# First batch of x loaded as f32 on two hardware queues and cast on chip, in a fused cross-attention and PReLU layer

## The chip, the cores and the metric

The kernel runs on one core of one Trainium2 chip. Its time is the device time of one execution in microseconds; with several runs, the median. A core has five engines, each with an instruction stream of its own: TensorE (PE) multiplies, VectorE (DVE) and ScalarE (ACT) do elementwise work and empty PSUM, GpSimd (POOL) does elementwise work on SBUF, SyncE (SP) only issues transfers. Transfers (DMAs) run on 16 DMA engines that all queues share. A queue belongs to the engine that issues: SyncE and ScalarE have hardware queues, GpSimd has a software queue. Here only GpSimd's transfers change the type on the way (f32 in HBM to f16 in SBUF).

## What is computed

With 8 batches, 8 heads, 512 tokens, 32 states and 64 values a head, tokens read from states and states read from tokens, and every row then goes through a two-layer PReLU network:

```python
scores = scale * x @ state.T;  a  = softmax(scores);  xread = a @ state
scores2 = scale * state @ x.T; a2 = softmax(scores2); sread = a2 @ x
rows = concat([xread, sread], axis=2)          # 8 * (512 + 32) rows of 512
h = rows @ w_in                                # 512 -> 2048
g = max(h, 0) + alpha * min(h, 0)
out = g @ w_out                                # 2048 -> 512, f32
```

## The kernel before

Inputs are f32, matmuls work on f16. Since `xread` is `a @ state`, the kernel folds the states into the first layer: `m = state @ w_in` for each batch (steps `m`, in four blocks of 512 columns of w_in, L445), evicted to SBUF by `mo` (L467), and `h = m.T @ a.T` directly (steps `F`, or half by half `f`). The rows of `sread` are gathered in `XS` and go through the network at the end as a ninth batch.

The work is a list of steps. The string `ORDER` names them in program order; each engine executes its own instructions in that order, and a wait holds up everything behind it on its engine. Nothing else schedules: the pools are under a manual schedule. A token such as `xt.0.1.0.2` is the step `xt` with its arguments; the last number of many tokens is the PSUM bank ("place") k0 to k5 that it writes, and letters a, v, p choose ScalarE, VectorE or GpSimd for a copy.

Steps for one batch b, in the order in which they need each other:

- `lx` loads x of the batch with a cast (L162); batch 0 has `lx0`, in two halves of four heads (L179). `xt` transposes it on TensorE, four heads and one of two token halves at a time (L281), `xo` evicts (L286). From batch 2 on `xd`, a DMA transpose on SyncE's queue, does both (L273).
- `sc` makes all scores in PSUM (L295). Batch 0 works first in two halves of four heads (`sc.0.0`, `sc.0.1`).
- State softmax for the tokens: `sb` transposes 32x32 blocks on VectorE (L330), `smax` (L336), `ssh` subtracts on GpSimd (L342), `sexp` on ScalarE (L348), `ssum` with the reciprocal on VectorE (L352, L353), `snorm` multiplies on GpSimd (L356), `wb` transposes back (L364). The result is the weights that `F` and `f` stream.
- Token softmax for the states: `tm` (L376), `te` (L387), `tsum` (L397), `tn` on GpSimd (L401), `tt`, a DMA transpose of the result e2T on SyncE's queue (L405), `rd` the matmuls (L420).
- `F.b.jc` (L478) and `f` (L499) make one `h` of 128 of the 2048 hidden values for 512 tokens; `N` (ScalarE, L510) and `G` (VectorE, L518) are the PReLU; `S.b.q.i` (L530) adds two hidden blocks to the output of 128 tokens, `O` evicts (L568) and stores (L571).

`wi` and `wo` load w_in and w_out in four blocks each, on GpSimd's queue, with a cast (L198, L204); `lst` loads the states of batches 1 to 7 (L192), `str` and `sro` transpose and evict them (L232, L263). The states of batch 0 come as f32 on SyncE's queue (L172), are cast (`stc`, L238), transposed (`stt`) and evicted (`sto`, L246). `oma` turns alpha into 1 - alpha, a column for each hidden block (L251, L252). `Z.k.n` multiplies zeros n times on TensorE (L217); its results are not used.

GpSimd's queue begins with x of batch 0 in two halves, then the states, w_in block 0, x of batch 1, w_in block 1. The rest of w_in and w_out and x of batch 2 follow between GpSimd's own steps.

Of the kernel before, what the change touches and what calls it, by code (L numbers as in the profile page):

```python
# [26 lines left out]
S.0.0.1 S.0.1.1 G.0.5 mo.4.0.a.0 tn.0.1 m.0.2.0.3 sc.1 G.0.7 S.0.2.0.5 mo.0.2.a.0 tm.1 m.1.2.0.4  # L27
wo.2 tn.0.0 mo.0.2.a.1 mo.1.2.a.0 S.0.2.1 lx.2 wo.3 sb.1 F.0.6.3 F.0.9.0 mo.1.2.a.1 N.0.6 S.0.2.2
S.0.0.2 N.0.9 G.0.6 S.0.1.2 smax.1 te.1.1 te.1.0 F.0.11.4 G.0.9 ssh.p.1 F.0.8.3 N.0.8 N.0.11 S.0.0.3
S.0.1.3 m.0.3 G.0.8 F.0.10.0 mo.0.3.a.0 N.0.10 sexp.1 S.0.2.3 mo.0.3.v.1 xd.2 G.0.11 G.0.10  # L30
S.0.3.0.3 m.1.3 S.0.3.1 mo.1.3.a.0 F.0.14.4 S.0.2.4 F.0.13.0 N.0.14 tt.0 ssum.1 S.0.0.4 S.0.1.4
S.0.0.5 S.0.3.2 G.0.14 F.0.12.4 N.0.13 G.0.13 F.0.15.0 snorm.p.1 N.0.12 N.0.15 mo.1.3.a.1 wb.1
S.0.3.3 S.0.1.5 S.0.3.4 G.0.12 S.0.2.5 G.0.15 S.0.3.5 F.1.2.4 S.0.2.6 N.1.2 F.1.0.0 tsum.1 S.0.2.7
N.1.0 S.0.1.6 S.0.1.7 G.1.2 O.0.2.a sc.2 m.2.1.4.5 S.0.0.6 O.0.1.a F.1.7.2 mo.2.1.a.0 mo.2.1.a.1
G.1.0 F.1.1.0 tm.2 sb.2 F.1.3.4 N.1.7 S.0.0.7 S.0.3.6 N.1.1 G.1.1 N.1.3 tn.1.0 O.0.0.a te.2.0
F.1.5.5 S.0.3.7 N.1.5 G.1.3 F.1.9.0 S.1.1.0.1 G.1.7 F.1.4.4 smax.2 O.0.3.a S.1.1.1 tn.1.1 G.1.5
rd.0.2 te.2.1 N.1.9 G.1.9 m.2.3 F.1.6.3 N.1.4 rdo.0.a F.1.12.5 N.1.6 lx.3 G.1.4 F.1.13.2 N.1.12
F.1.8.0 G.1.6 G.1.12 S.1.2.0.4 N.1.13 G.1.13 ssh.p.2 N.1.8 S.1.1.2 F.1.11.3 G.1.8 F.1.10.5 N.1.11
S.1.2.1 N.1.10 G.1.11 G.1.10 S.1.2.2 sexp.2 S.1.1.3 ssum.2 F.1.14.2 F.1.15.0 snorm.p.2 mo.2.3.a.0
S.1.1.4 mo.2.3.a.1 S.1.1.5 m.3.2 m.4.2.3.5 N.1.14 tt.1 tsum.2 N.1.15 G.1.14 mo.3.2.a.1 S.1.1.6  # L40
S.1.2.3 S.1.2.4 mo.3.2.a.0 mo.4.2.a.0 G.1.15 mo.4.2.a.1 S.1.2.5 S.1.1.7 xd.3 O.1.1.a m.3.1.2.0
m.2.2.3.5 sc.3 wb.2 tn.2.1 S.1.2.6 S.1.2.7 mo.3.1.a.1 F.2.15.1 S.1.0.0.0 mo.2.2.a.0 mo.3.1.a.0
O.1.2.a lx.4 mo.2.2.a.1 sb.3 N.2.15 S.1.0.1 tm.3 F.2.13.3 N.2.13 G.2.15 S.1.0.2 F.2.4.2 tn.2.0
F.2.2.4 G.2.13 smax.3 N.2.4 F.2.9.5 F.2.0.1 N.2.9 S.1.0.3 S.1.0.4 G.2.9 S.1.0.5 N.2.2 N.2.0 te.3.0
F.2.12.3 S.1.0.6 N.2.12 G.2.2 G.2.4 G.2.0 xd.4 F.2.7.5 G.2.12 S.1.3.0.4 ssh.p.3 sexp.3 N.2.7 ssum.3
S.1.0.7 te.3.1 F.2.3.2 S.1.3.1 F.2.1.1 N.2.3 S.1.3.2 N.2.1 F.2.8.3 G.2.3 S.1.3.3 G.2.1 S.1.3.4
# [59 lines left out]
def kernel(  # L106
# [106 lines left out]
    def zeros(k, n):  # L213
        t = single(k, f"z_{len(zs)}", [128, 128], F32)
        zs.append(t)
        for _ in range(n):
            nc.tensor.matmul(t, zero, zero, start=True, stop=True)  # L217
# [422 lines left out]
```

## Time and profile before

| what | us |
|---|---|
| median of 3 runs (lowest, highest) | 218.81 (218.28, 219.42) |
| the profiled execution's own time | 219.05 |
| its span, first to last instruction | 217.3 |
| TensorE busy | 210.2 |
| VectorE, ScalarE, GpSimd busy | 166.5, 137.6, 71.1 |
| the granted TensorE clock | 1.000 |
| zeros on TensorE (L217), 82 instructions | 7.5 |
| GpSimd's queue, share of 16 DMA engines | 28.2% |

Busy times are added up for each engine over the span; engines run side by side. A line of the timeline has the start, the time, the engine, the line, the operation, what it writes and reads, how many were merged, and in brackets how long the engine was idle before and what ended that. In the rows by slices a digit is the busy share in tenths. DMA rates count the bytes written, so a transfer that casts f32 to f16 counts half of what it reads.

### The profile page before, as it was taken

The numbers are of one execution on the slowest core, as the hardware profiler recorded it, in microseconds if no ns is written. First come the engines' busy times: TensorE is split into PE (matmuls) and PEld (weight loads), VectorE is DVE, ScalarE is ACT, GpSimd is POOL, SyncE is SP. The second block draws the span as 40 slices with busy tenths as digits, with TensorE's granted clock in tenths as the row PEclk, the third lists the DMA queues.
The fourth block names the chain that finished last, engine by engine and source line by source line (L and its number), as shares of the span: only waits on it lengthen the run. The fifth ranks groups of instructions, "written<-read, shape, count | busy, mean of one in ns | idle before, by whom it ended". The sixth has DMA issues, their size and how long they took to land.

```text
span 217.3 us, 4317 instructions
## 1 busy us (share of the span) xinstructions
PE 210.2 (97%) x1698; PEld 104.0 (48%) x1698; DVE 166.5 (77%) x255; ACT 137.6 (63%) x271; POOL 71.1 (33%) x58
## 2 busy tenths in 40 slices
PE   7979999999999999999999999999999999999994
PEld 7753334444443544544444445444454455554453
DVE  2789998899899899798998869977898466665001
ACT  3498984899988848885857937565545346544021
POOL 7491943730943703191336310902500000000000
PEclk9999999999999999999999999999999999999999
DMA  6999999599196494159922311051240111100124
GB/s 88 173 198 208 195 195 176 139 203 136 54 139 147 53 227 111 51 99 193 236 52 100 97 50 51 0 100 48 50 149 9 40 51 48 48 37 11 51 97 145
DMA packets 39716, 23.12 MB, mean 106 GB/s; under 512 B 22144, under 2 KB 35984, under 8 KB 39696
## 3 DMA queue, kind: packets, MB, share of 16 engines
q0 software_dynamic: 12704, 8.62, 28.2%
q1 hardware_dynamic: 26960, 14.23, 26.5%
q8 instruction: 13, 0.21, 0.4%
q14 instruction: 7, 0.06, 0.1%
q10 hardware_dynamic: 32, 0.01, 0.0%
HBM read 17.31 MB, written 8.91 MB: 121 GB/s over the span
## 4 chain that ended last, share of the span: by engine, by line
PE 87%; DMA 8%; POOL 2%; issue 1%; DVE 1%; ACT 0%; POOLq 0%
PE o L530 48%; PE h L478 24%; DMA w_in_sb<-in_moe_w_in_dram 5%; PE m_ps L445 4%; PE h L487 3%; PE o L578 3%; DMA xT<-xg 3%; PE o L550 2%; PE sr_ps L420 2%; PE sc L295 1%; DVE m L467 1%; POOL xg L179 1%; POOL xg L162 0%; PE h L499 0%; POOL w_in_sb L198 0%
## 5 line engine op out<-in xcount | busy, mean ns | idle before, releaser
L530 PE MATMUL o<-w_out_sb,gt 128*128 128x512 f16 x496 | 125.3, 379 | 0.0
L510 ACT ACTIVATE neg<-h 128x512 f32<-128x512 f32 (+1 forms) x144 | 76.9, 577 | 46.9 <-PE h L478 37.4
L518 DVE SCALAR_TENSOR_TENSOR gt<-neg,oma_sb,h 128x512 f16<-128x512 f32 x128 | 89.9, 738 | 15.8 <-ACT neg L510 14.7
L530 PEld LDWEIGHTS <-gt 128*128 128x128 f16 x496 | 47.3, 98 | 55.4 <-issue 3.4
L478 PE MATMUL h<-aT,m 128*128 128x512 f16 x250 | 68.3, 379 | 0.0
L478 PEld LDWEIGHTS <-m 128*128 128x128 f16 x250 | 24.1, 98 | 28.4 <-issue 0.6
L401 POOL TENSOR_SCALAR e<-e,r 128x512 f16<-128x512 f16 x16 | 25.0, 1568 | 21.1 <-DVE r L397 17.5
L467 ACT CAST m<-m_ps 128x512 f16<-128x512 f32 x50 | 27.0, 603 | 5.0 <-PE m_ps L445 4.6
L356 POOL TENSOR_TENSOR an<-ts,r 128x1024 f16<-128x1024 f32 (+1 forms) x9 | 15.5, 1720 | 33.9 <-DVE r L353 14.8
L342 POOL TENSOR_TENSOR ts<-ts,mx 128x1024 f32<-128x1024 f32 (+1 forms) x9 | 15.5, 1721 | 28.5 <-DVE mx L336 28.5
L568 ACT COPY osb<-o 128x512 f32<-128x512 f32 x22 | 12.9, 591 | 14.9 <-PE o L530 14.9
L445 PE MATMUL m_ps<-w_in_sb,stT 64*32 64x512 f16 x256 | 11.3, 383 | 0.9 <-DMA w_in_sb<-in_moe_w_in_dram 0.7
L387 ACT ACTIVATE e<-sc,nb 128x512 f16<-128x512 f32 x16 | 11.1, 700 | 1.1 <-DVE nb L379 1.1
L364 DVE STREAM_TRANSPOSE aT<-an 128x1024 f16<-128x1024 f16 (+1 forms) x9 | 10.1, 1120 | 1.8 <-POOL an L356 1.8
L518 DVE SCALAR_TENSOR_TENSOR gs<-neg,oma_sb,h 128x256 f16<-128x256 f32 x16 | 7.5, 478 | 4.5 <-ACT neg L510 4.5
L467 DVE CAST m<-m_ps 128x512 f16<-128x512 f32 x14 | 9.1, 679 | 2.1 <-ACT m L467 1.6
L352 DVE TENSOR_REDUCE r<-ts 128x32 f32<-128x1024 f32 (+1 forms) x9 | 9.9, 1095 | 0.0
L336 DVE TENSOR_REDUCE mx<-ts 128x32 f32<-128x1024 f32 (+1 forms) x9 | 9.8, 1092 | 0.0
L376 DVE TENSOR_REDUCE nb<-sc 128x2 f32<-128x1024 f32 x8 | 9.6, 1204 | 0.3 <-PE sc L295 0.3
L487 PE MATMUL h<-XS,w_in_sb 128*128 128x256 f16 x64 | 9.4, 273 | 0.0
L588 DVE COPY osr<-o 128x512 f32<-128x512 f32 x1 | 0.7, 691 | 11.3 <-PE o L578 11.3
L217 PE MATMUL z<-zero 128*128 128x128 f16 x82 | 7.5, 262 | 1.4 <-DVE zero L211 1.1
(51 smaller groups left out, 127.0 us busy)
## 6 DMA issues: line engine op xcount, KB each, us to landing
out_dram<-osb SPq DMA_DIRECT2D x27, 256.0 KB, 2.2
xg<-in_x_dram POOLq DMA_DIRECT2D x7, 512.0 KB, 6.8
w_in_sb<-in_moe_w_in_dram POOLq DMA_DIRECT2D x4, 512.0 KB, 9.3
w_out_sb<-in_moe_w_out_dram POOLq DMA_DIRECT2D x4, 512.0 KB, 8.8
out_dram<-osb SPq DMA_DIRECT2D x9, 128.0 KB, 2.0
xg<-in_x_dram POOLq DMA_DIRECT2D x2, 256.0 KB, 4.2
out_dram<-osr SPq DMA_DIRECT2D x2, 256.0 KB, 3.1
st<-in_state_dram POOLq DMA_DIRECT2D x1, 224.0 KB, 4.8
```

The lines of the kernel that those rows point to most:

```text
L342: engine(e).tensor_tensor(ts, ts, over_blocks(cols(live["mx", b], j, S // N)), ALU.subtract)
L356: engine(e).tensor_tensor(blocks(cols(live["an", b], j, S)), blocks(cols(live["ts", b], j, S)), over_blocks(cols(live["r1", b], j, S // N) ...
L387: nc.scalar.activation(live["e2", b][:, g, :, :], live["sc", b][:, :, :, g, :].rearrange("p r j s -> p (r j) s"), EXP, bias=live["nb", b][ ...
L401: nc.gpsimd.tensor_scalar_mul(e2, e2, live["r2", b][:, g : g + 1])
L445: nc.tensor.matmul(t[N * k : N * (k + 1), :], st_head(b, h)[64 * r : 64 * r + 64, :], w_in_sb[64 * r : 64 * r + 64, c, 512 * f : 512 * (f ...
L467: copier(e)(m_tile(b)[:, f, g, :], live["mp", b, f][g])
L478: nc.tensor.matmul(h.rearrange("p (r j s) -> p r j s", r=2, j=2), ms[b][:, f, g, 128 * j : 128 * (j + 1)], weights(b, g), start=(g == 0), ...
L487: nc.tensor.matmul(h, w_in_sb[:, c, 128 * jc : 128 * (jc + 1)], XS[:, c].rearrange("p q n b -> p (q n b)"), start=(c == 0), stop=(c == n_c ...
L510: nc.scalar.activation(neg, h, RELU, bias=0.0, scale=-1.0)
L518: nc.vector.scalar_tensor_tensor(gt, negs.pop((b, jc)), oma_sb[:, jc : jc + 1], h, ALU.mult, ALU.add)
L530: nc.tensor.matmul(outs[b, q], gts[b, jc][:, 128 * q : 128 * (q + 1)], w_out_sb[:, jc, :], start=(jc == 0), stop=(jc == n_jc - 1),)
L568: copier(e)(osb, t)
```

## The change

- x of batch 0 is loaded as f32 into a buffer of its own (a tile of the pool of m), in four pieces: heads 0 to 2 and 4 to 5 on SyncE's queue, head 3 and heads 6 to 7 on ScalarE's. Steps `xc` cast it to f16: heads 0 to 2 on VectorE, 3 and 4 to 5 on ScalarE, 6 to 7 on GpSimd.
- The states of batch 0 go from SyncE's to ScalarE's queue, with two rows of 64 next to each other for each partition; their eviction undoes that order. alpha goes from ScalarE's to SyncE's queue.
- GpSimd's queue begins with the states of batches 1 to 7, w_in block 0 and x of batch 1; its cast of heads 6 to 7 stands ahead of w_in block 1.
- `Z` multiplies up to 512 columns in one instruction, n counts units of 128 columns. 82 instructions become 21.
- The order of steps is new up to batch 2, and the PSUM places are new in the whole program; from batch 3 on the order is the same. On TensorE `m.1.1` and `m.0.1` stand ahead of the first `f`; on VectorE `ssum.0.1` stands behind `xo.1.0.0`; on GpSimd `tn.0` stands behind `ssh.p.1`; on SyncE `tt.0` stands ahead of `xd.2`.
- The outputs of batch 2 are stored in one transfer instead of two.

```diff
-stc lx0.0 lx0.1 oma id Z.1.20 stt.0 Z.2.18 xt.0.0.0.1 sto.a xt.0.1.0.2 xo.0.0.0.v lst xo.0.1.0.v
-Z.0.6 sc.0.0 xt.0.1.1.3 xt.0.0.1.4 sb.0.0 xo.0.0.1.v smax.0.0 xo.0.1.1.a str.0.5 sc.0.1 str.1.0 wi.0
-sro.0.a lx.1 wi.1 ssh.p.0.0 sb.0.1 Z.1.3 sc.0 Z.5.7 m.0.0.1.2 sro.1.a sexp.0.0 smax.0.1 m.3.0.3.4
-ssh.p.0.1 tm.0 mo.0.0.a.1 sexp.0.1 ssum.0.0 m.1.0.5.0 ssum.0.1 te.0.1 te.0.0 mo.1.0.v.1 wo.0
-mo.1.0.a.0 snorm.p.0.0 mo.3.0.a.1 Z.2.28 xt.1.1.1.2 xt.1.1.0.5 mo.0.0.a.0 snorm.p.0.1 wb.0.0
-mo.3.0.a.0 m.2.0 xt.1.0.1.0 xo.1.1.0.v xt.1.0.0.4 f.0.0.0.1 f.0.1.0.5 wi.2 mo.2.0.a.0 wb.0.1
-mo.2.0.a.1 f.0.1.1 xo.1.0.0.v N.0.1 m.0.1.3.4 f.0.0.1 mo.0.1.a.1 m.1.1 xo.1.1.1.v N.0.0 xo.1.0.1.v
-mo.0.1.v.0 f.0.2.0.2 F.0.3.0 f.0.2.1 F.0.4.3 mo.1.1.v.0 mo.1.1.a.1 F.0.7.4 G.0.1 N.0.2 G.0.0 wo.1
-F.0.5.5 N.0.3 G.0.2 wi.3 m.4.0 N.0.4 S.0.0.0.1 N.0.5 G.0.3 tsum.0 S.0.1.0.2 N.0.7 mo.4.0.a.1 G.0.4
...
+xc.1.a stc lst id xc.0.v wi.0 Z.1.28 stt.0 lx.1 Z.2.8 xt.0.0.0.1 sto.v xc.3.p xo.0.0.0.v xc.2.a oma
+xt.0.1.0.2 xo.0.1.0.a Z.0.5 str.1.3 sc.0.0 sro.1.a xt.0.1.1.4 xt.0.0.1.5 wi.1 xo.0.1.1.a sb.0.0
+str.0.0 xo.0.0.1.v sc.0.1 smax.0.0 m.0.0.1.2 sro.0.a mo.0.0.a.1 wo.0 m.2.0.3.5 mo.0.0.a.0 sb.0.1
+ssh.p.0.0 sc.0 smax.0.1 m.1.0.4.0 ssh.p.0.1 tm.0 sexp.0.0 mo.1.0.a.1 mo.2.0.a.0 sexp.0.1 Z.2.20
+xt.1.0.0.2 xt.1.1.0.1 ssum.0.0 te.0.1 xo.1.0.0.v ssum.0.1 m.3.0.0.3 te.0.0 wi.2 mo.3.0.a.0
+xt.1.0.1.2 mo.3.0.a.1 snorm.p.0.0 mo.2.0.v.1 mo.1.0.a.0 Z.0.18 m.1.1.0.5 wb.0.0 m.0.1 f.0.0.0.3
+snorm.p.0.1 mo.1.1.a.1 wb.0.1 f.0.1.0.4 f.0.1.1 F.0.3.5 mo.1.1.a.0 xo.1.0.1.v xt.1.1.1.2 f.0.0.1
+f.0.2.0.0 N.0.1 mo.0.1.v.0 mo.0.1.a.1 xo.1.1.0.v G.0.1 f.0.2.1 F.0.5.1 N.0.0 N.0.3 m.4.0 xo.1.1.1.v
+wo.1 G.0.0 N.0.2 F.0.4.4 F.0.7.2 S.0.1.0.3 N.0.5 mo.4.0.a.0 wi.3 G.0.3 S.0.0.0.5 G.0.2 N.0.4 G.0.5
...
-    nc.sync.dma_start(st0_32, rows[:n0, :].rearrange("(g p) d -> p g d", p=128))
+    x32 = moe.tile([128, H, 2, 2, D], F32, name="x32", tag="m", bufs=7)
+    heads = ((0, 3), (3, 4), (4, 6), (6, 8))
...
-    nc.scalar.dma_start(al32[:n_jc, :], moe_alpha.rearrange("(jc p) -> jc p", p=128))
+
+    def load_x32(engine, i):
+        lo, hi = heads[i]
+        engine.dma_start(
+            x32[:, lo:hi].rearrange("p k j r d -> p k (j r d)"),
+            x[0, lo:hi].rearrange("k (p j r) d -> p k (j r d)", j=2, r=2),
+        )
+
+    load_x32(nc.sync, 0)
+    nc.sync.dma_start(al32[:n_jc, :], moe_alpha.rearrange("(jc p) -> jc p", p=128))
+    nc.scalar.dma_start(st0_32, rows[:n0, :].rearrange("(p g) d -> p g d", g=2))
+    load_x32(nc.scalar, 1)
+    load_x32(nc.sync, 2)
+    load_x32(nc.scalar, 3)
...
-    def load_x0(g):
...
+    def x0_cast(i, e):
+        lo, hi = heads[i]
+        copier(e)(xgs[0][:, lo:hi], x32[:, lo:hi])
...
-    zero = consts.tile([128, 128], F16)
+    zero = consts.tile([128, 512], F16)
...
-        for _ in range(n):
-            nc.tensor.matmul(t, zero, zero, start=True, stop=True)
+        while n:
+            w = 128 * min(n, 4)
+            nc.tensor.matmul(t[:, :w], zero[:, :128], zero[:, :w], start=True, stop=True)
+            n -= w // 128
...
-        w = 256 if b == 2 else 512
-        for c in range(0, d_model, w):
-            nc.sync.dma_start(rows[:, c : c + w], osb[:, c : c + w])
+        nc.sync.dma_start(rows, osb)
```

More of the change, by code (lines that the diff above doesn't have):

```diff
@@ L29 @@
[L29 to L34, printed above, removed]
@@ new lines @@
+F.1.13.4 xd.3 F.1.10.2 m.2.3 G.1.6 N.1.13 G.1.11 S.1.1.2 N.1.8 ssh.p.2 F.1.14.5 S.1.1.3 N.1.10
+S.1.2.0.3 mo.2.3.a.0 G.1.13 S.1.2.1 sexp.2 G.1.10 S.1.2.2 F.1.15.4 G.1.8 ssum.2 S.1.1.4 mo.2.3.a.1
+S.1.2.3 m.3.2 N.1.14 m.4.2.2.1 G.1.14 mo.4.2.v.0 mo.3.2.a.0 S.1.2.4 N.1.15 snorm.p.2 S.1.1.5
+mo.3.2.a.1 mo.4.2.a.1 S.1.2.5 G.1.15 wb.2 S.1.1.6 S.1.2.6 m.2.2.5.2 m.3.1.4.1 sc.3 S.1.2.7
+mo.3.1.v.0 mo.2.2.a.1 F.2.13.2 lx.4 mo.2.2.a.0 S.1.0.0.4 N.2.13 sb.3 S.1.0.1 F.2.12.5 tsum.2
+mo.3.1.a.1 O.1.2.a S.1.1.7 G.2.13 F.2.4.1 N.2.12 smax.3 S.1.0.2 G.2.12 F.2.9.2 O.1.1.a F.2.2.3 N.2.9
@@ new lines @@
+F.2.15.0 N.2.2 S.1.0.3 tm.3 F.2.0.5 S.1.0.4 tn.1.1 ssh.p.3 N.2.15 S.1.0.5 tt.1 N.2.4 G.2.2 G.2.9
+N.2.0 G.2.15 sexp.3 G.2.0 S.1.0.6 G.2.4 F.2.3.3 F.2.7.2 ssum.3 N.2.7 xd.4 S.1.3.0.0 S.1.3.1 S.1.0.7
+F.2.1.5 tn.2.1 N.2.1 N.2.3 F.2.8.1 G.2.1 S.1.3.2 G.2.3 tn.2.0 S.1.3.3 N.2.8 te.3.1 S.1.3.4 S.1.3.5
+te.3.0 O.1.0.a S.1.3.6 G.2.7 F.2.6.5 N.2.6 m.3.3.3.2 G.2.8 sc.4 rd.1.4 snorm.p.3 F.2.5.1 G.2.6
+mo.3.3.a.0 F.2.14.3 rdo.1.a wb.3 N.2.5 tsum.3 S.2.1.0.5 F.2.11.4 mo.3.3.a.1 G.2.5 S.1.3.7 N.2.14
+F.2.10.2 F.3.4.1 G.2.14 N.2.11 S.2.1.1 F.3.1.3 lx.5 O.1.3.v N.3.4 S.2.1.2 N.2.10 G.2.11 tt.2
@@ new lines @@
+tsum.4 snorm.p.4 F.3.5.3 mo.4.3.a.0 mo.4.3.a.1 F.3.0.5 F.3.10.0 N.3.0 S.2.3.7 O.2.3.a S.2.2.0.2
+S.2.2.1 F.3.11.1 G.3.0 wb.4 S.2.2.2 S.3.3.0.4 F.3.15.5 S.3.3.1 N.3.5 lx.6 G.3.5 te.5.0 te.5.1 N.3.10
+N.3.15 S.2.2.3 F.3.12.3 S.2.2.4 N.3.11 S.3.3.2 lx.7 N.3.12 G.3.10 G.3.15 F.4.6.0 N.4.6 tn.4.0
+F.4.5.5 G.3.11 F.4.3.1 N.4.5 S.2.2.5 G.3.12 G.4.5 S.3.3.3 F.4.4.3 S.3.3.4 F.4.7.5 N.4.4 S.3.3.5
+S.2.2.6 N.4.3 sb.5 N.4.7 S.3.3.6 S.2.2.7 G.4.4 G.4.7 S.3.3.7 F.4.1.3 F.4.0.5 xd.6 O.2.2.a S.3.1.0.2
+O.3.3.a S.3.1.1 F.4.9.4 N.4.1 smax.5 G.4.6 N.4.0 S.3.0.0.0 tn.4.1 S.3.0.1 G.4.1 G.4.0 F.4.8.3
@@ new lines @@
+N.4.14 F.4.12.2 G.4.14 O.3.2.a sexp.6 tn.5.1 S.4.1.0.0 m.6.3 m.7.2.4.5 m.5.2.1.3 mo.6.3.v.0 S.4.1.1
+mo.5.2.v.0 mo.7.2.a.0 S.4.1.2 mo.5.2.a.1 F.5.15.4 mo.6.3.v.1 mo.7.2.a.1 tt.5 S.4.1.3 N.5.15 G.5.15
+F.4.15.1 F.5.12.3 S.4.1.4 F.5.5.5 N.4.12 F.5.13.4 S.4.1.5 N.5.12 N.4.15 G.4.12 tsum.6 G.4.15
+S.4.0.0.2 S.4.1.6 S.4.1.7 N.5.5 S.4.0.1 S.4.2.0.1 O.4.1.v G.5.5 S.4.0.2 F.5.10.0 N.5.13 F.5.1.5
+S.4.2.1 G.5.12 F.5.0.3 N.5.10 S.4.0.3 S.4.2.2 S.4.0.4 G.5.13 tn.6.1 N.5.0 G.5.10 N.5.1 G.5.1
+m.6.1.4.0 m.7.0 mo.6.1.a.1 mo.6.1.a.0 S.4.0.5 mo.7.0.v.0 S.4.0.6 F.5.2.5 N.5.2 S.4.0.7 mo.7.0.v.1
@@ L245, in first_states_out @@
     def first_states_out(e):
-        copier(e)(stT[:, :n0], live.pop("st0_ps").rearrange("d g p -> d (g p)"))
+        copier(e)(
+            stT[:, :n0].rearrange("d (p g) -> d p g", g=2),
+            live.pop("st0_ps").rearrange("d g p -> d p g"),
+        )
     def one_less_alpha():
```

122 lines of the change are left out of this document (50 added, 72 removed).

## The prediction

> **What bounds the kernel now.** I read the engine shares and the slices first, then the chain of work that ended last in order of time, then the DMA queues and the timeline of the first 24 us.
>
> ```profile
> PE 210.2 (97%) x1698; PEld 104.0 (48%) x1698; DVE 166.5 (77%) x255; ACT 137.6 (63%) x271; POOL 71.1 (33%) x58
> ...
> PE   7979999999999999999999999999999999999994
> ```
>
> TensorE is full from the third slice of 5.4 us on. The real matmuls behind the start are the same before and after, so only the moment from which TensorE runs without gaps can move the end, and stalls that the new order makes later. The chain, 0 to 40 us (start, length, what):
>
> ```profile
> 4.82 0.87 POOL xg L162
> 5.68 11.78 DMA w_in_sb<-in_moe_w_in_dram
> 17.46 0.04 issue
> 17.50 0.41 PE m_ps L445 x8
> ```
>
> Up to 17.46 us the chain is the second block of w_in, queued on GpSimd's queue behind x of batch 0, the states, the first block and x of batch 1; after it every step is TensorE's. The DMA view of 0 to 20 us (slices of 0.5 us) says when that queue runs:
>
> ```profile
> DMA  0001416999999999999999999999999999999999
> GB/s 0 0 0 45 103 6 67 179 199 192 196 164 133 165 191 138 174 205 203 207 189 114 168 196 224 186 200 201 205 213 203 201 207 209 207 209 201 209 203 213
> ...
> q0 software_dynamic: 4135, 3.17, 105.9%
> ```
>
> The engines start on it at 3.0 us, need one slice (67 GB/s) to get going, and never rest again; the 64 KB of the first states, on SyncE's queue, came at 1.5 to 2.5 us. The timeline:
>
> ```profile
> 1.23 1.72 POOL L179 DMA_DIRECT2D xg<-in_x_dram  x2 [0.80 <-POOLq L624]
> ...
> 5.84 0.90 PE L281 MATMUL xT_ps<-ident,xg 128*128 128x128 f16 x8
> ...
> 12.39 1.72 PE L217 MATMUL z<-zero 128*128 128x128 f16 x28 [0.28 <-ACT m L467]
> ...
> 15.00 0.62 PE L281 MATMUL xT_ps<-ident,xg 128*128 128x128 f16 x8 [0.88 <-DMA xg<-in_x_dram]
> ...
> 16.35 0.81 PE L499 MATMUL h<-aT,m 128*128 128x512 f16 x3
> 17.50 0.41 PE L445 MATMUL m_ps<-w_in_sb,stT 64*32 64x512 f16 x8 [0.34 <-DMA w_in_sb<-in_moe_w_in_dram]
> ...
> 21.11 1.90 PE L530 MATMUL o<-w_out_sb,gt 128*128 128x512 f16 x8
> ```
>
> x of batch 1 lands at 14.96 us (issued at 4.80), the first `h` starts at 16.35, the first output matmul (S) at 21.11. I take S as the marker: what it gains is gained at the end, unless a later wait eats it.
>
> **The change part by part.**
>
> *x of batch 0 on the hardware queues.* SyncE issued at 0.73 us and its packets ran from about 1.8 (slice 1.5 to 2.0); GpSimd issued at 1.23 and its packets ran from 3.0. So the stream starts 1.1 us earlier; the slow first slice (67 against about 200 GB/s, 0.35 us) now lies under other packets; the 64 KB of states join the stream (+0.2). The transfer itself writes 1 MB of f32 where it wrote 512 KB of f16. No row shows such a load. Below: a w_in block, 1 MB of f32 read, takes 2.54 us (17.46 to 20.0, the next landing). Above: if written bytes were what counts, 1 MB at the 205 GB/s of the cast stream is 5.1 us. The nearest rows are the hardware queue's own between 40 and 60 us:
>
> ```profile
> GB/s 0 0 225 307 365 152 30 73 93 160 123 126 172 236 319 371 339 224 93 195 304 56 4 9 243 291 244 0 0 0 0 0 0 0 0 0 238 287 17 66
> ```
>
> 365 GB/s while only output writes ran: 2.9 us for 1 MB. I take 3.0, against about 3.5 for both halves before (3.0 to 6.5 us). Then x of batch 1 (L) lands 1.1 + 0.35 + 0.5 - 0.2 = 1.75 us earlier, at 13.2; ends 12.7 and 15.3. Everything behind it in GpSimd's queue shifts alike, w_in block 1 to about 15.7.
>
> [...]
>
> *Casts.* Four copies: DVE 768 wide, ACT 256 and 512, GpSimd 512. Rows: 0.28 us for 128 elements on DVE (L238), 0.37 and 0.59 on ACT (L246, L467), 1.05 for a 512-wide two-input op on GpSimd (L342). DVE's is then 0.6 to 0.95, GpSimd's 0.5 to 1.05. Heads 0 to 3 land at 3.5 to 5 us (sharing with the states, which GpSimd issues at 1.23), heads 4 to 7 at 5.2 to 7; cast, 4.4 to 5.9 and 6.1 to 8. The transposes cannot use the early end: the first 28 units of zeros, 107 ns for 128 columns there (20 in 2.31 us, the last one 0.31 long), take 3.0 us from 1.2, and four state transposes (0.42) and 8 more units (0.86) keep TensorE busy to 5.5, against 5.84 before. The first scores come at about 7.2 (7.32 before). What covers all of this is the wait for L: TensorE idles about 1.6 us before it. With heads 4 to 7 a whole us later the cover is gone and 0.4 us shows. GpSimd's cast waits for them with w_in block 1, w_out block 0 and the score shifts queued behind it; the engines are busy with earlier blocks until 13, so the issue at 7 to 9 us costs nothing.
>
> *Zeros.* 82 instructions of 128 columns become 21 of up to 512: 10,496 columns against 10,112. Costs nothing, they stand in waits.
>
> *The new order before S.* TensorE now has both m matmuls of w_in block 1 ahead of the first `h`; DVE has the second half's sum (L352) behind the eviction of batch 1's first transposes, so it waits for L, and with it wait an eviction of m and both transposes back to weights behind it on DVE, and the first `h` that need these. From L: transposes and hop 0.45, eviction 0.42, sum and reciprocal 0.94 (0.69 + 0.25), GpSimd's product 1.04 (L356), transpose back 0.70 (L364), in all 3.55. The w_in way is as long: 2.5 for the block, 0.8 for two m groups, 0.45 for two `h`. Then, to S: `h` matmuls at 0.215 each, 12 of them (2.6), four transposes 0.3, m of batch 4 0.4, switches 0.25: 3.55. S is at L + 7.1 = 20.3, 0.8 us earlier. Before it was 6.15 behind L: what the order gains (the w_in block waits at 17.50) it partly gives to the sum's wait.
>
> *Behind S.* SyncE has the DMA transposes in the other order:
>
> ```profile
> 32.98 3.37 SPq L273 DMA_TRANSPOSE xT<-xg  x1
> 36.40 1.30 SPq L405 DMA_TRANSPOSE e2T<-e  x1
> ```
>
> Now e2T goes first, and it waits for GpSimd's two products (L401, 1.57 each), which moved behind the shift of batch 1 (28.34 before, 1.9 long): shift from 27.6, products to 32.8, e2T issue 1.3, x of batch 2 issued at 34.1. The six such transposes land 5.2 us after issue in the median: 39.3; the first took 6.1, beside the last w_out block (landing at 36.6, now about 35). TensorE gets to the scores that need it (40.43 before) at about 39.2. Cost 0.1, with ends 0 (4.3 us) and 0.9 (6.1 us). Output of batch 2 in one DMA for two: four issues of 0.33 us less on a SyncE that waits; nothing. New PSUM places and the states' layout (512 B rows): nothing, the same sizes are evicted.
>
> **Sum.** -0.8 + 0.1 = -0.7 us. The profiled execution took 219.05 us (span 217.3, 1.75 around it), so 218.35; the median shown is 218.81, 0.24 less than that execution, so 218.1 as a median.
>
> **The rivals.**
> - *Only the start.* The queues take turns without gain: x costs its 3.5 us as before, the slow slice stays, and L moves by the earlier start less the 64 KB alone, 14.96 - 1.1 + 0.2 = 14.06; S at 21.15, no gain, with the 0.1 above 218.9. For it: the cast queue's share is already 105.9%. Against: the 365 GB/s.
> - *More.* Hardware packets fill gaps of the cast stream, x costs 2.5 and heads 4 to 7 land by 6: L at 12.7 or below, w_in block 1 at 15.2, S at 19.7 to 19.9: 217.4. For it: 164 and 133 GB/s at 5.5 to 6.5 us show gaps to fill. Against: S then needs the shift chain of the first half to be on time too.
> - *Late transposes.* x of batch 2 takes 6.1 us again: +0.8 on the forecast, 218.9.
> - *Slower: written bytes count.* x at 205 GB/s takes 5.1 us; L at 15.3, w_in block 1 at 17.8, S at 22.4: +1.3, with the scores' wait 220.2. It decides from 4.1 us for x on (L at 14.3). For it: no row shows an f32 load from HBM of that size, and the cast stream never passes 224 GB/s. Against: 365 for outputs.
>
> **How the numbers follow.** Chances: forecast 0.30, only the start 0.10, late transposes 0.08, more 0.28, slower 0.24. 0.5% of this kernel, 1.1 us, is about what a measurement can tell from no change; the first three lie within it. Faster 0.28, same 0.48, slower 0.24. The range takes in "more" (217.4, 217.0 with its bounds) and "written bytes" (220.2): 217.0 to 220.2; the forecast's own is 217.6 to 218.9.
>
> **What would show it.** Packets of the hardware queues from 1.8 us at over 300 GB/s; batch 1's first transposes at 13.2; the second sum on DVE directly behind them; first `h` at about 16.6 and S at 20.3; e2T issued near 32.8, x of batch 2 near 34.1, its scores waiting little. I am wrong if L comes after 14, if heads 4 to 7 hold up the first-batch softmax, or if TensorE waits at scores 2 for longer than 0.5 us.

## The result and the profile after

The changed kernel takes 219.53 us (22 executions, 219.20 to 222.39) against 218.79 us (22, 218.04 to 219.42): ratio 1.0054, 95% interval 1.0036 to 1.0071. I forecast 218.1, so the sign is wrong; the range (217.0 to 220.2) holds the median. 16 of the 22 lie between 219.20 and 219.67 (median 219.44, so the loss is not the clock's alone); the other six are those with a mean granted TensorE clock of 0.984 to 0.992, and five of them take 220.18 to 222.39. No execution of the kernel before that was timed beside the experiments has a clock below 0.998. The profiled execution is one of the six (220.92, span 219.1), so what belongs to the clock has to be kept apart below.

The page of the kernel after: engine shares, slices and clock.

```profile
PE 209.8 (96%) x1637; PEld 99.4 (45%) x1637; DVE 167.7 (77%) x258; ACT 137.6 (63%) x271; POOL 70.1 (32%) x57
...
PE   7498999999999999999999999999999999999994
...
PEclk9969999999999999999999999999999999999999
```

The second slice (5.4 to 10.9 us) has fallen from 9 to 4 tenths, and the clock is not full in the third. The chain of work that ended last, 0 to 40 us (start, length, what), says what TensorE waits for:

```profile
1.76 7.07 DMA x<-in_x_dram
8.83 0.02 issue
8.85 0.62 ACT xg L194
9.47 0.49 ACT xT L303
9.96 0.04 issue
10.00 0.30 PE sc L312 x8
...
17.37 0.48 ACT m L484
17.86 0.04 issue
17.90 1.15 PE z L230 x5
19.05 0.04 issue
19.09 0.45 PE m_ps L462 x8
```

Before, the chain led through GpSimd's queue to block 1 of w_in and from 17.5 us on through TensorE. Now it starts with heads 4 and 5 of x of batch 0, which land 7.07 us after their issue, goes through their cast on ScalarE to an eviction, also on ScalarE, and only then to the first scores, at 10.00. Between 10 and 17.9 us more than half of it is ScalarE's. And it goes through `z`, zeros. The timeline of TensorE:

```profile
7.03 0.58 PE L246 MATMUL st_ps<-ident,st 128*64 128x128 f16 x14 [0.22 <-DMA st<-in_state_dram]
...
10.00 0.30 PE L312 MATMUL sc<-xT,stT 64*32 64x256 f16 x8 [2.39 <-ACT xT L303]
...
17.90 1.13 PE L230 MATMUL z<-zero 128*128 128x512 f16 x5 [0.87 <-ACT m L484]
19.09 0.63 PE L462 MATMUL m_ps<-w_in_sb,stT 64*32 64x512 f16 x16
19.64 0.82 PE L516 MATMUL h<-aT,m 128*128 128x512 f16 x3
...
23.35 1.97 PE L547 MATMUL o<-w_out_sb,gt 128*128 128x512 f16 x8
```

In the kernel before, the first scores ran at 7.32, on an eviction by VectorE:

```profile
7.32 0.30 PE L295 MATMUL sc<-xT,stT 64*32 64x256 f16 x8 [0.24 <-DVE xT L286]
```

TensorE now waits 2.39 us ahead of the first scores, where it waited 0.24. S is at 23.35 (21.11 before). The DMA view of 0 to 20 us, which shows that the stream as a whole did what was wanted:

```profile
DMA  0002039999999999999999999999999999999998
GB/s 0 0 0 26 0 70 307 362 366 258 237 280 362 356 246 217 213 207 200 195 196 201 200 200 206 206 205 209 209 201 203 213 238 190 193 205 207 209 209 133
```

The stream moves 237 to 366 GB/s from 3.0 to 7.5 us, and x of batch 1 (L) lands at 13.21, block 1 of w_in at 15.74: to the tenth what I had forecast. What failed is that L no longer decides S.

### The profile page after: what moved, and what is told of

It reads as the page before. It is cut to its first block, busy times and chain, and to the rows that moved or that the text cites. A ratio compares the mean times of both kernels' runs of the same rounds, so it can differ in the third digit from the quotient of the medians.

```text
span 219.1 us, 4198 instructions
## 1 busy us (share of the span) xinstructions
PE 209.8 (96%) x1637; PEld 99.4 (45%) x1637; DVE 167.7 (77%) x258; ACT 137.6 (63%) x271; POOL 70.1 (32%) x57
## 4 chain that ended last, share of the span: by engine, by line
PE 85%; ACT 7%; DMA 3%; DVE 2%; issue 1%; SPq 0%
PE o L547 47%; PE h L495 23%; PE m_ps L462 3%; DMA x<-in_x_dram 3%; PE h L504 3%; PE o L593 3%; ACT m L484 2%; ACT neg L527 2%; PE o L567 2%; PE sr_ps L437 2%; ACT e L404 1%; PE sc L312 1%; DVE m L484 1%; DVE ts L345 1%; PE z L230 1%
## 5 line engine op out<-in xcount | busy, mean ns | idle before, releaser
L535 DVE SCALAR_TENSOR_TENSOR gt<-neg,oma_sb,h 128x512 f16<-128x512 f32 x128 | 89.9, 737 | 16.2 <-ACT neg L527 15.4
L484 ACT CAST m<-m_ps 128x512 f16<-128x512 f32 x48 | 26.5, 599 | 7.1 <-PE m_ps L462 6.8
L462 PE MATMUL m_ps<-w_in_sb,stT 64*32 64x512 f16 x256 | 12.2, 405 | 0.7 <-ACT stT L280 0.4
L484 DVE CAST m<-m_ps 128x512 f16<-128x512 f32 x16 | 10.4, 677 | 1.7 <-ACT m L484 1.3
L381 DVE STREAM_TRANSPOSE aT<-an 128x1024 f16<-128x1024 f16 (+1 forms) x9 | 10.1, 1120 | 1.3 <-POOL an L373 1.1
L365 ACT ACTIVATE ts<-ts 128x1024 f32<-128x1024 f32 (+1 forms) x9 | 8.7, 964 | 0.2 <-POOL ts L359 0.2
```

Of the source, the lines that this page charges most:

```text
L462: nc.tensor.matmul(t[N * k : N * (k + 1), :], st_head(b, h)[64 * r : 64 * r + 64, :], w_in_sb[64 * r : 64 * r + 64, c, 512 * f : 512 * (f ...
L484: copier(e)(m_tile(b)[:, f, g, :], live["mp", b, f][g])
L535: nc.vector.scalar_tensor_tensor(gt, negs.pop((b, jc)), oma_sb[:, jc : jc + 1], h, ALU.mult, ALU.add)
```

## The experiments

In each edit the tokens of the order are shown with their neighbours. S is the first output matmul of the profiled execution, as in the prediction.

**1. The eviction ahead of the cast.**

```diff
-xc.3.p xo.0.0.0.v xc.2.a oma xt.0.1.0.2 xo.0.1.0.a Z.0.5
+xc.3.p xo.0.0.0.v oma xt.0.1.0.2 xo.0.1.0.a xc.2.a Z.0.5
```

> The changed kernel with one step moved: on ScalarE the eviction of the first half's second token half stands ahead of the cast of heads 4 and 5. Theory (late heads): heads 4 to 7 land at 8.5 to 8.8 us whatever stands on ScalarE, and the cast held up the first scores, which ran at 10.0. They now run at 7.6 (behind the state transposes that wait for the states at 7.0); the second half's scores, which need heads 4 to 7, come at about 10.8 instead of 11.6, so S comes only 0.7 to 0.9 us earlier than with the same clock before, and the time is 218.5 to 218.9. Rival (order behind): the sums, the m matmuls and the DMA transposes in their new places set the time; 219.4 to 219.6, unchanged. Rival (one wait): the cast ahead of the eviction was all that went wrong; then S = 20.5 to 21 and 217.9 to 218.3.

218.82 us (218.72 to 219.26), ratio to the kernel before 1.0010 (0.9998 to 1.0022). The first scores run at 7.42, the second half's at 10.33, S at 21.53; one of 12 executions has a clock of 0.992. So one token on ScalarE was most of what the change had lost, in part by way of the clock (run 9, which holds the clock and leaves the token where it is, has 1.0034): it is the theory's case, with the time at its upper end. The forecast's 218.1 is still 0.7 away. The chain of this kernel, 0 to 30 us, where TensorE comes in only at 16 us:

```profile
1.75 6.38 DMA x<-in_x_dram
...
8.16 0.62 ACT xg L194
8.78 1.05 ACT stT L280
9.83 0.44 ACT xT L303
10.28 0.97 ACT stT L280
11.25 0.94 ACT m L484 x2
12.19 0.53 ACT ts L365
12.72 0.96 ACT m L484 x2
13.68 0.53 ACT ts L365
14.21 1.34 ACT e L404 x4
15.55 0.48 ACT m L484
...
16.08 1.15 PE z L230 x5
...
17.27 0.45 PE m_ps L462 x8
```

ScalarE works from 8.16 to 16.04 without a gap: a cast, two evictions of states, one of x, five of m, the two exponentials of the first batch (`ts`) and the token softmax's (`e`). L, at 13.2, is in no link of it. And TensorE, which waited for ScalarE, first multiplies zeros for 1.15 us before it makes m of batch 1, whose block of w_in had landed at 15.72.

**2. Ten matmuls of zeros where TensorE was idle.**

```diff
-Z.0.5 str.1.3 sc.0.0
+Z.0.5 str.1.3 Z.0.40 sc.0.0
```

> The changed kernel with 40 more units of zeros on TensorE (10 matmuls 512 wide, 0.21 us each at the full clock) between the state transposes and the first scores, where TensorE was idle from 7.6 to 10.0 us. Nothing else moves. Theory (late heads, clock on top): the first scores still run at 10.0, no execution shows a granted clock below 1, the spread shrinks to 219.1 to 219.7, the median is 219.3 to 219.5: the drop cost only what the executions above 219.8 show. In the profile S is at 22.2 to 22.7. Rival (the clock is all of it): the median falls to 218.2 to 218.7. Rival (the clock falls for another reason than the idle time): executions at 220 to 222 are still there.

220.22 us (219.81 to 220.44), clock 1.000 in all six. The spread is gone, as the theory says, but the median is 0.7 above its 219.3 to 219.5. The reason is in the landings: in this execution heads 4 to 7 landed at 7.74 and 7.92, not 8.5 to 8.8, so the scores could have run near 9 (an estimate: 7.92, the cast of 0.62 and the eviction of 0.49), and the zeros held them to 9.92. Too many zeros; run 9 has fewer.

**3. GpSimd's queue silent until x has landed.**

```diff
-xc.1.a stc lst id xc.0.v wi.0 Z.1.28
+xc.1.a stc id xc.0.v xc.3.p lst wi.0 Z.1.28
```

> The changed kernel with GpSimd's cast of heads 6 and 7 put ahead of all transfers on GpSimd's queue, so that the 1 MB of f32 x, the 64 KB of first states and alpha have the DMA engines to themselves: the disputed cost alone. Theory (shared engines): the hardware queues move 300 KB/us or more, and heads 4 to 7 land at 5.2 to 5.8 us instead of 8.5 to 8.8; the first scores then wait for the states (transposed ahead of them), x of batch 1 lands at 15.5 or later, the time is 220 to 223. Rival (the load is slow by itself, from many short rows or from two queues): heads 4 to 7 land at 7.5 or later with nothing beside them.

One execution: 223.24 us. Heads 6 and 7 land at 6.56, heads 4 and 5 at 6.93: between the two expectations. The DMA view of 0 to 10 us, in slices of 0.25 us, of this kernel:

```profile
GB/s 0 0 0 0 0 0 0 82 64 20 63 217 285 324 377 377 383 379 385 389 334 295 266 131 94 25 0 0 0 0 0 0 0 0 57 79 100 79 151 201
```

and of the changed kernel:

```profile
GB/s 0 0 0 0 0 0 0 51 0 0 4 135 295 320 336 387 387 344 273 244 235 239 226 333 356 367 381 332 254 238 221 213 217 209 209 205 205 195 189 201
```

Alone, the f32 load runs at 377 to 389 GB/s for about 1.5 us, near the rate that I had taken (365). But the packets that come at 1.75 us carry only 20 to 82 GB/s; the load proper begins at 2.75 us, from 5.75 us on it trickles (131, 94, 25 GB/s), and the last piece lands at 6.93. So from first packet (1.78) to last landing it is 5.1 us alone, and beside GpSimd's queue 7 us in the profiled execution (landings at 8.46 and 8.83); in runs 1, 2 and 9, with the same loads, the last landing is at 7.92 to 8.18.

**4. Wide zeros and one store for batch 2, on the kernel before.**

```diff
-    zero = consts.tile([128, 128], F16)
+    zero = consts.tile([128, 512], F16)
...
-        w = 256 if b == 2 else 512
-        for c in range(0, d_model, w):
-            nc.sync.dma_start(rows[:, c : c + w], osb[:, c : c + w])
+        nc.sync.dma_start(rows, osb)
```

> The kernel before with two parts of the change alone: zeros 512 columns wide and the outputs of batch 2 in one transfer. Theory: both cost nothing, 218.5 to 219.1, clock 1.0. Rival (the wide zeros matter, by the clock or by delaying what stands behind them): 219.4 or more, or some executions with a clock below 1.

218.64 us, ratio 1.0003 (0.9986 to 1.0020), clock 0.997 or more: these two parts cost nothing that the interval shows. A side result: here x of batch 1 landed at 14.01 and S was at 20.71, with the same load as before (14.01 in run 6 too). The execution of the kernel before that I had read (L 14.96, S 21.11) was the later one; against this one, L gains 0.8 us by the change and not 1.75.

**5. No zeros ahead of m.1.1,** on top of run 1.

```diff
-mo.2.0.v.1 mo.1.0.a.0 Z.0.18 m.1.1.0.5 wb.0.0
+mo.2.0.v.1 mo.1.0.a.0 m.1.1.0.5 wb.0.0
```

> The changed kernel with the eviction ahead of the cast (as in the run that moved that step alone, 218.82) and, besides, without the 18 units of zeros that stand on TensorE ahead of m.1.1. There TensorE waited for ScalarE until 16.08, multiplied zeros for 1.15 us, and only then made m of batch 1, whose block of w_in had landed at 15.72. Theory (ScalarE is late and the zeros stand behind it, on the path): m.1.1 at 16.1, the first h at 16.8 to 17.0, S at 20.4 to 20.8 instead of 21.53, time 217.8 to 218.2. Rival (the weights from GpSimd and VectorE set the first h, and the evictions of m behind them S): the first h at 17.4 or later, S at 21.1 to 21.5, time 218.5 to 218.9.

218.84 us, ratio 1.0030 (1.0005 to 1.0055), of two groups: seven executions at full clock take 218.26 to 218.91, five with a clock of 0.990 to 0.992 take 219.85 to 220.51. In the profiled one the first h is at 16.72 and S at 20.75, as the theory has it; its time of 217.8 to 218.2 is missed even at full clock (median of the seven: 218.60). So the zeros were on the path, and they were not idle either: without them five of 12 executions have a lower clock, and these take 1.8 us longer (their median is 220.41).

**6. The load undone, the order kept.** The four loads and casts go; `lx0`, as in the kernel before, stands first on GpSimd's queue.

```diff
-xc.1.a stc lst id xc.0.v wi.0 Z.1.28
+stc lx0.0 lx0.1 id lst wi.0 Z.1.28
```

> The changed kernel with the load undone: x of batch 0 again in two halves with a cast, first on GpSimd's queue; the new order, zeros and stores stay, and the four casts on chip go. Theory (the late landing of heads 4 to 7 started the loss, the order with its evictions and zeros ahead of the first h adds to it): heads land at 5.2 and 6.8, the first scores run at 7.4 to 7.6, the second half at 8.9 to 9.3, x of batch 1 lands at 14.6 to 15.0 and block 1 of w_in at 17.1 to 17.5; the first h stands behind m.1.1, which needs that block, so at 18.0, S at 21.6 to 21.9: 219.0 to 219.5. Rival (the load alone made it slower): S at 21.0 to 21.2, 218.4 to 218.8, as before. Rival (the order alone made it slower): S at 22.2 or later, 219.5 or more.

220.55 us, ratio 1.0099 (1.0078 to 1.0120): worse than theory, and the rival "the order alone". S at 22.82; five of six executions have a clock of 0.989 to 0.992, the sixth takes 220.31. I had not seen why: the new order puts a transposition of the later states ahead of the first scores, and with the old load these states land at 8.73.

```profile
8.77 0.58 PE L235 MATMUL st_ps<-ident,st 128*64 128x128 f16 x14 [2.04 <-DMA st<-in_state_dram]
9.29 0.30 PE L301 MATMUL sc<-xT,stT 64*32 64x256 f16 x8
```

The order is made for a queue that begins with the states, so this run gives no price of the order by itself.

**7. Half and half.** Heads 4 to 7 by GpSimd with a cast, first on its queue; no zeros ahead of m.1.1.

```diff
-xc.1.a stc lst id xc.0.v wi.0 Z.1.28
+xc.1.a stc lx0 id xc.0.v lst wi.0 Z.1.28
...
-    load_x32(nc.sync, 2)
-    load_x32(nc.scalar, 3)
```

> The changed kernel with heads 4 to 7 loaded with a cast by GpSimd, first on its queue, and only heads 0 to 3 as f32 on the hardware queues; no casts of heads 4 to 7 on chip, and no zeros ahead of m.1.1. Theory (late heads): with half the f32 rows, heads 4 to 7 land at 6.0 to 6.8, the first scores at 7.4 to 7.6 and those of the second half at 9.0 to 9.5; x of batch 1 at 13.2 to 13.8, S at 20.0 to 20.6, time 217.3 to 218.0. Rival (the hardware queues slow whatever stands beside them, so heads 4 to 7 still come at 7.5 or later): S at 20.8 to 21.4, 218.2 to 218.7.

219.86 us, ratio 1.0070 (1.0045 to 1.0096); two executions at full clock take 219.16 and 219.20, four with 0.990 to 0.992 take 219.64 to 220.85. Heads 4 to 7 land at 6.90, but the first scores run at 9.11: as in run 6 the states (8.56) hold them up. I missed that a second time; both of its theories fell to it.

**8. The new load with the order of before** from the second half's scores on, and 8 units of zeros for 28 ahead of x of batch 1 (the lines of the changed kernel that these replace are left out).

```diff
+xt.0.1.0.2 xo.0.1.0.a Z.0.5 sc.0.0 str.0.5 sb.0.0 sro.0.a xc.2.v smax.0.0 xt.0.1.1.3 xt.0.0.1.4 xo.0.0.1.v
+xo.0.1.1.a sc.0.1 str.1.0 wi.1 ssh.p.0.0 sb.0.1 Z.1.3 sc.0 Z.5.7 m.0.0.1.2 sro.1.a sexp.0.0 smax.0.1
...
+mo.3.0.a.1 Z.2.8 xt.1.1.1.2 xt.1.1.0.5
```

> The new load with the order of before from the second half's scores on (with the start reordered: the eviction ahead of the cast, heads 4 and 5 cast on VectorE, one state transposition and its eviction while TensorE waits for heads 4 to 7; 8 units of zeros instead of 28 ahead of x of batch 1). Theory (the new order's ScalarE work, sums and zeros ahead of the first h are a part of the loss): heads 4 to 7 land at 8.0 to 8.8, the second half's scores at 9.8 to 10.4, x of batch 1 at 13.2, the first h at 15.5 to 16.2, S at 20.0 to 20.6, 217.4 to 218.0. Rival (late heads set everything through the second half's softmax, whatever the order): S at 21.0 to 21.6, 218.4 to 219.0.

220.04 us, ratio 1.0060 (1.0035 to 1.0085): four executions at full clock, 218.46 to 219.14, seven with 0.981 to 0.992, 219.90 to 221.57. S at 20.74, between the two expectations. Full clock or not, this order is no better than that of run 1 (the four at full clock have a median of 218.94, run 1 has 218.82).

**9. Five matmuls of zeros instead of ten,** in the changed kernel.

```diff
-Z.0.5 str.1.3 sc.0.0
+Z.0.5 str.1.3 Z.0.20 sc.0.0
```

> The changed kernel with 20 units of zeros, five matmuls of 0.21 us at the full clock, between the state transposes and the first scores: they end near 8.7 us, ahead of the scores, which come at 9.1 at the earliest. Theory (the clock is granted anew every 3.41 us, by how busy TensorE was in the 3.41 us before; the traces so far show the half clock behind stretches in which it was busy for 0.12 to 0.33, and the full one from 0.38 on): no such stretch is left, no execution has a clock below 0.998, the slow executions of the changed kernel (220 to 222.4) are gone and the rest is as it was: 219.2 to 219.7, median 219.3 to 219.5. Rival (zeros in front of the scores cost time by themselves, as ten matmuls did with 220.2): median 219.8 or more. Rival (the clock falls for something else): executions of 220 and more with a clock near 0.99 remain.

219.56 us (219.28 to 219.83), ratio 1.0034 (1.0019 to 1.0048), all 12 at 0.999 or more. Theory: the executions above 220 are gone, and the rest is where it was, though the median lies just above its 219.5. The shares in the expectation count only the time in which columns stream (512 in about 0.21 us, as the prediction's `h` matmuls at 0.215). In the profile's own busy time, which the view by stretches gives, the same reads like this. Three stretches of 3.41 us of the changed kernel (length, TensorE busy, weight loads, VectorE, ScalarE, GpSimd, clock, DMA):

```profile
4.04:7.46 3.42, 2.44 (x32) 1.23 (x30) 2.19 (x8) 0.41 (x1) 0.18 (x1) 1.00 1.13 301
7.46:10.87 3.41, 1.02 (x24) 0.73 (x20) 0.74 (x3) 2.02 (x4) 2.06 (x3) 1.00 1.31 204
10.87:14.29 3.42, 3.02 (x62) 1.24 (x63) 2.81 (x6) 3.12 (x6) 1.69 (x2) 0.50 1.34 204
```

of run 3, which fell twice over:

```profile
4.71:8.12 3.41, 1.58 (x16) 0.68 (x12) 2.21 (x8) 1.51 (x3) 1.51 (x3) 1.00 0.34 117
8.12:11.53 3.41, 0.41 (x8) 0.41 (x10) 0.00 (x0) 0.00 (x0) 2.97 (x4) 0.50 0.90 129
11.53:14.95 3.42, 3.42 (x58) 2.06 (x52) 1.99 (x4) 2.23 (x3) 0.42 (x1) 0.50 1.24 172
14.95:18.36 3.41, 2.95 (x61) 1.41 (x53) 3.29 (x6) 3.41 (x8) 2.41 (x3) 1.00 1.32 199
```

and one of run 7, which did not fall:

```profile
7.45:10.86 3.41, 1.88 (x44) 1.49 (x45) 1.37 (x4) 1.64 (x3) 0.00 (x0) 1.00 1.25 201
```

In the changed kernel's trace the clock changes at 10.87, 14.29 and 219.09 us, 3.41 and 204.80 us apart: once and 60 times such a stretch. It falls to half behind 1.02 us of work in 3.41 (1.37 in run 6, 1.58 in run 3), at 219.09 behind 0.47, and stays half behind 0.41 (run 3); it is full again behind 3.02 us (3.02 in run 6, 3.42 in run 3). In the other profiles the stretches of this length that I read have 1.88 us (run 7), 1.95 (run 8), 2.00 (run 5) and more, and the clock stays full. The fall begins at 10.87 us here, at 9.54 in run 6, at 8.12 in run 3. Why the same kernel is hit in some executions only is not shown: no two traces here show one kernel both ways.

**10. Zeros where TensorE waits,** on top of run 5.

```diff
-Z.0.5 str.1.3 sc.0.0 sro.1.a xt.0.1.1.4
+Z.0.5 str.1.3 sc.0.0 sro.1.a Z.0.12 xt.0.1.1.4
...
-xt.1.0.1.2 mo.3.0.a.1
+Z.2.16 xt.1.0.1.2 mo.3.0.a.1
```

> The kernel with the eviction ahead of the cast and no zeros ahead of m.1.1 (median 218.84, of two groups: seven executions of 218.26 to 218.91 at full clock and five of 219.85 to 220.51 with a clock of 0.990 to 0.992), now with zeros where TensorE waits: 12 units behind the first scores and 16 units ahead of the last early transposition of batch 1, both ending before what they stand ahead of is ready. Theory (busy share by stretches of 3.41 us): the second group is gone, all executions at 218.2 to 219.0, median 218.4 to 218.7, which is no gain over the kernel before. Rival (the zeros ahead of m.1.1 were only in the way, and the second group has another cause): the second group stays, median near 218.9 or above.

218.32 us (217.86 to 218.87), ratio 0.9973 (0.9961 to 0.9986), clock 0.999 or more in all 12: the second group is gone, as the theory says. The theory's "no gain" is not borne out here, but see run 12. In this execution block 1 of w_in ends a wait again: GpSimd issues it behind the cast of heads 6 and 7, it lands 8.30 us later, and TensorE waits 0.80 us for it ahead of m.1.1:

```profile
7.80 0.56 POOL xg L194
8.36 8.30 DMA w_in_sb<-in_moe_w_in_dram
...
16.71 0.46 PE m_ps L462 x8
```

**11. Half and half once more,** on top of run 10, the state transposition behind the first scores.

```diff
-xo.0.1.0.a xc.2.a Z.0.5 str.1.3 sc.0.0 sro.1.a Z.0.12 xt.0.1.1.4 xt.0.0.1.5 wi.1 xo.0.1.1.a
+xo.0.1.0.a Z.0.5 sc.0.0 Z.0.4 xt.0.1.1.4 xt.0.0.1.5 wi.1 str.1.3 xo.0.1.1.a sro.1.a
...
-sc.0.1 smax.0.0 m.0.0.1.2
+sc.0.1 smax.0.0 Z.2.24 m.0.0.1.2
```

> The kernel with zeros in the waits (median 218.32), with heads 4 to 7 loaded with a cast by GpSimd, first on its queue, as in the half-and-half run, but with the state transposes behind the first scores, so that the states' landing at 8.6 holds up nothing ahead of them; 24 units of zeros fill the wait for block 0 of w_in. Question: does the late landing of heads 4 to 7 (7.7 to 8.2, and two casts) still cost something there? Theory (it does: the second half's softmax sets the weights): heads 4 to 7 land at 6.6 to 7.0, the second half's scores run at 8.9 to 9.3 instead of 10.1 to 10.3, the weights and the first h come 0.3 us or more earlier than 17.27, time 217.7 to 218.1. Rival (ScalarE's row of evictions, and x of batch 1 and block 1 of w_in, which now land 0.5 us later, set the first h): first h at 17.2 to 17.8, 218.3 to 218.9.

218.77 us, ratio 1.0004 (0.9991 to 1.0017). Heads 4 to 7 land at 7.31, the second half's scores run at 9.37 (10.13 in run 12), each 0.1 to 0.3 later than the theory's; x of batch 1 lands at 13.62, block 1 of w_in at 16.69, and the first h is at 17.29, behind a wait of 0.60 us for that block: the rival. How much of this is the price of the load stays open. The block landed at 16.66 in run 10 too, without the half load, and the 17.27 that the theory set out from was that block's wait and not the weights'. And the second half's scores were not free of the states: TensorE waited 0.48 us for them (8.42) and transposed all of them ahead of these scores.

**12. Run 10 again,** beside run 11.

> The kernel with zeros in the waits once more, on the same chip as the half-and-half version next to it. Theory: the gain is repeatable, 0.996 to 0.999 of the kernel before, no execution with a clock below 0.998. Rival (the gain was that chip's): the interval takes in 1.

218.36 us (217.74 to 218.66), ratio 0.9993 (0.9982 to 1.0004), clock 1.00. Its own time repeats to 0.04 us, but the kernel before took 218.54 beside it, where it had taken 218.89 beside run 10. So the interval takes in 1, as the rival has it, and what can be said is that this version is not slower than the kernel before and at best some 0.3% faster, and clearly faster than the changed kernel (ratio 1.0054, and 1.0034 in run 9). Run 12's chain of work that ended last, 0 to 22 us:

```profile
1.76 6.18 DMA x<-in_x_dram
...
7.96 0.62 ACT xg L194
...
14.01 1.35 ACT e L404 x4
...
15.44 1.06 POOL an L373
...
16.52 0.72 DVE aT L381
...
17.29 0.38 PE h L516
```

Zeros and blocks of w_in are out of it in this execution. What is left is x of batch 0, ScalarE without a gap from 7.96 to 15.36, the product on GpSimd and the transposition back to weights; L (12.89) and block 1 of w_in (15.43) wait for it, not it for them. In run 10, the same kernel, the block landed 1.2 us later, and then TensorE waited for it: the two paths are nearly as long, and the landing decides which one ends last.

## Why the prediction was wrong

- **The stream and L: right in number, in part by accident.** L at 13.21 (forecast 13.2) and block 1 of w_in at 15.74 (15.7). The term "x of batch 0 takes 3.0 us" was mis-sized: 5.1 us from first packet to last landing alone, 7 beside GpSimd's queue in the profiled execution. The rate was right for the middle of the load, 377 to 389 GB/s; I had left out a slow first us and the landing, and I had let the stream start at 1.8 us where only thin packets do. That it came out even for L is, as I read the DMA view, because GpSimd's queue filled what the hardware queues left (never under 195 GB/s from 3.0 us until L); no run shows it by itself. My first rival put what the queues take from each other into L (14.06). The runs show it in x: it landed at 6.9 alone (run 3), and beside GpSimd's queue at 8.8 in the profiled execution and at 7.7 to 8.2 in the profiles of the other runs with this load.
- **"The first scores come at about 7.2": the step that failed first.** I had heads 4 to 7 landing at 5.2 to 7; they landed at 8.5 to 8.8 in the profiled execution. I had named the price of a late landing (0.4 us when a whole us late), but only for what needs heads 4 to 7. I had not looked at what stands behind their cast on ScalarE: the eviction of the first half, which does not need them, and for which the first scores wait. They came at 10.00, and moving that one step takes the ratio from 1.0054 to 1.0010 (run 1), and from 1.0034 if the clock is held (run 9).
- **"What covers all of this is the wait for L": wrong.** The cover was real before. After it, ScalarE works through from the landing of heads 4 and 5 to 16 us, so each tenth that it starts late is a tenth late at the end (run 1's chain). I costed the casts and evictions as durations, not as a row on one engine.
- **"TensorE is full from the third slice of 5.4 us on": misread.** The row has 7 tenths in the third slice and is full from the fourth (16.3 us) on. The sum does not rest on it.
- **"Zeros cost nothing, they stand in waits": wrong in place, and wrong in what they do.** Their width costs nothing (run 4, 1.0003). But 18 units stand behind a wait for ScalarE and ahead of m.1.1: 1.13 us of TensorE on the path. No wait in the trace before shows it; the order that comes with the change does.
- **"S is at L + 7.1": wrong.** (The w_in way that I called as long as 3.55 adds up to 3.75, so my own terms gave up to L + 7.3.) It was L + 10.1 in the profile after, L + 8.9 without the fall of the clock (run 9: L 13.2, S 22.10), L + 8.35 with the eviction moved, L + 7.65 in run 12. My sum began at L, and in the changed kernel L no longer ended any wait.
- **The clock: not in the prediction at all.** The profile before showed a mean of 1.000, and I took that for a constant, though my own row of the start, 107 ns for 128 columns of zeros, stood beside 28 such units in 1.72 us (0.06 each) at 12.39. In the traces the half clock lasts 3.41 us (the profile after and run 6) or 6.83 (run 3), and TensorE was not idle in the 3.41 us ahead of it: it had worked for 1.02, 1.37 and 1.58 us. The clock is the smaller part of the median: with the clock held (run 9) the ratio is 1.0034 instead of 1.0054, intervals that overlap. All executions of the changed kernel above 220 have a clock of 0.984 to 0.992.
- **Behind S: better than forecast.** I had +0.1 us. From S to the end of the span it took 196.16 us before and 195.79 after (195.82 in run 9, 195.78 in run 10): the 0.2 us wait for the transposed x of batch 2 is gone. The rest is not explained: run 4, with the order of before, has no such wait and takes 196.08, and runs 5, 7 and 11, with the new one, take 196.01 to 196.10. The transposes came in the order that I had given, e2T issued at 36.36 and x of batch 2 at 37.89, landed 4.4 us later (5.2 forecast); both were late by more than S (e2T 3.6 us), and still no wait shows.
- **The base.** I measured the gain from one execution of the kernel before, whose L was 14.96; with the same load L was 14.01 in run 4 and S 20.71. Against that one, 0.8 of the 1.75 us by which L was to come earlier were there to be had, and that L met its 13.2 is luck to that extent.
- **The rivals.** "Slower: written bytes count" had the sign, a time (220.2) and nearly a length for x (5.1 us) that fit, but not the mechanism: alone, the load ran at up to 389 GB/s and took its 5.1 us by a slow start and a slow end, and L did not come late. The real rival, a wait on ScalarE in front of the first scores, was not among mine. My own list of what would make me wrong had it: "if heads 4 to 7 hold up the first-batch softmax".

What stays open: which part of ScalarE's row from 8 to 15.4 us could go elsewhere. The load of fewer heads as f32 did not help (run 11), but block 1 of w_in and the states stood in its way, so the price of the late heads is not separated there. Why that block lands at 15.4 us in one execution and at 16.7 in the next is open too. And run 8, whose order has the exponentials of the first batch ahead of most evictions, let the clock fall in most executions, and was not run again with zeros in its waits.

## What to carry to other kernels

When a step that may be late is put on an engine, list what stands behind it there, also what has nothing to do with it: the cost of a late load is not its consumer's alone. When a load is to come earlier, ask in the chain of waits whether it still ends a wait once it does; here the bound went from a transfer to a full ScalarE, and in the changed kernel an L that was 0.8 to 1.75 us earlier bought nothing; with the zeros moved it was ScalarE in one execution (run 12) and a transfer in the other (run 10). And waits of TensorE in a start-up had a second price here besides their length: behind 3.41 us with 1.02, 1.37 and 1.58 us of work the next 3.41 us ran at half the clock, and behind 1.88 and more at the full one. It came in some executions and not in others, so a wider spread of times is itself a finding. Zeros in the waits, short enough to end before they did, took it away (run 10: 0.999 or more in all 12 executions, where five of 12 had 0.990 to 0.992 in run 5).

## What the runs showed of the hardware

- The granted clock fell to half for 3.41 us (profile after, run 6) or 6.83 us (run 3), behind 3.41 us in which TensorE was busy for 1.02, 1.37 and 1.58 us; in the other profiles it stayed full behind the stretches read, with 1.88 us (run 7) and more. The fall began at 10.87, 9.54 and 8.12 us. In run 5 the executions with a lower clock took 1.8 us longer by their medians; in run 1 the only one (0.992) took 0.4 us more than the median.
- The hardware queues started thin: issued at 0.72 us, packets from 1.78, but 20 to 82 GB/s until 2.75, then 217 and rising, to 377 to 389 from 3.5 on (run 3). The first packet of GpSimd's queue came at 4.3 us in the changed kernel's profile and at 3.7 to 3.8 in runs 1, 2, 9 and 11, issued at 1.24; before, with two small transfers on the hardware queues, it came at 2.9, issued at 1.23.
- The landing of the same load varied from execution to execution: heads 4 and 5 of the f32 load at 7.74 to 8.83 us, x of batch 1 with the old load at 14.01 or 14.96, block 1 of w_in in one and the same kernel at 15.43 or 16.66. A gain of some tenths is not read from one profile.
